# Every second attention head computed token-major, its probabilities turned by DMA, its value product four iterations later

## The chip, the cores and the metric

The kernel runs on one core of a Trainium2 chip. The metric is the device time of one execution in microseconds (us), as the median of repeated runs. The engines are named as the profile names them: PE (TensorE, matmuls), PEld (its weight loads), DVE (VectorE), ACT (ScalarE), POOL (GpSimd) and SP (SyncE, which here only issues DMAs; SPq is its queue). A matmul takes a stationary operand of 128x128 and streams a moving operand of up to 512 columns past it, into a PSUM bank of 512 f32 columns per partition. There are 8 banks.

## The reference

One transformer block with conditioning: a modulated layer norm, attention over the last 512 cached keys and values, an output projection, and a gated feed-forward part. It is cut here to the shapes that matter.

```python
# x [2048, 1024]; Hq = 32 heads of Dh = 128; 4 key/value heads; Sk = 2048; window W = 512; F = 3584; all bf16
sa, ca, ga, sb, cb, gb = split(silu(c) @ w_mod, 6)        # 6 rows of 1024
h = layernorm(x) * (1 + ca) + sa
q = (h @ wq) per head                                      # [32, 2048, 128]
k, v = last 512 rows of the caches, each shared by 8 heads
p = softmax(q @ k.T * Dh ** -0.5)                          # [32, 2048, 512]
x = x + ga * ((p @ v, heads joined) @ wo)
h = layernorm(x) * (1 + cb) + sb
x = x + gb * ((silu(h @ w_gate) * (h @ w_up)) @ w_down)
```

## The kernel before

The 2048 tokens are cut into 4 chunks of `CH` = 512 tokens. Attention runs over all chunks first, the feed-forward part follows. The residual `x_res` stays in SBUF throughout; nearly everything else lives in one arena that is carved by offsets (`arena.at`), where a new buffer takes over the pending reads and writes of those that it overlaps. A tracker (`T.op`) records the last writer and the readers of each buffer and emits the semaphore waits for them. The order of instructions on each engine is the order in which the Python code issues them; no scheduler changes it.

Attention is one loop, `for i in range(1, NA + 2)`, over `NA` = 128 heads in the order chunk, head (32 heads per chunk; head number i has chunk i // 32). It is a software pipeline. Iteration i does:

- `qproj(i + 3)`: 8 matmuls of 512 columns into bank 4 (`QB`), weights stationary, giving the query transposed (head dimension on partitions, tokens along the columns); DVE casts it to SBUF (L644).
- `scores(i - 1)`: 4 matmuls, one for each block of 128 keys, with the keys stationary and 512 query tokens moving, into banks 0 to 3. The result has keys on partitions. ACT takes the exponential of two banks at once (L813) into one of two buffers `ex_s`, 4 KB per partition.
- `pv(i - 2)`: the exponentials are the stationary operand, in pieces of 128 keys x 128 tokens, and the values with a column of ones appended are the moving one, 129 columns. 4 key blocks x 4 token blocks make 16 matmuls, into banks 5 and 6. The column of ones gives the softmax sum, and the output has tokens on partitions. DVE takes the reciprocal (L831) and scales (L834), and a DMA transpose issued from SP (L837) brings 128x512 into `oT_all`, the slot of that head.
- one step of background work (`run_bg`): the layer norm of the next chunk (statistics L424, normalisation L435, a DMA transpose of 128x1024 L454, modulation L440).
- loads: the query weights of four heads, 1 MB, every fourth iteration (`load_wq`); in chunks two and three, 24 columns of `w_mod` by DMA transposes of 256 KB (`load_mt`, L588) at the iterations of `LOADT`, each followed four iterations later by a multiply-and-sum on DVE (`mod_col`, L593).

After the last head of a chunk, `oproj` multiplies `oT_all` by the output weights: 8 blocks of 32 matmuls, 512 columns each, and DVE adds the residual by way of the `tmp` buffers (L853, L855). For the last chunk this is partly spread over the last iterations.

The feed-forward part has per chunk 28 blocks of 16 matmuls (`gateup`, with the Silu on ACT at L1059), and then `down`.

Of the kernel before, what the change touches and what calls it, by code (L numbers as in the profile page):

```python
# [3 lines left out]
ALU = mybir.AluOpType  # L4
AF = mybir.ActivationFunctionType
# [125 lines left out]
def bass_adaLN_cond__sliding_block_cached__swiglu_ffn__prompt_kernel(  # L131
# [63 lines left out]
    rstd = [rstd4[:, i:i + 1] for i in range(4)]  # L195
    bq = S_("bq", [P, 8], F32)
    rl = [S_("rl%d" % i, [P, 4], F32) for i in range(2)]
    nsc = [S_("nsc%d" % i, [P, D], BF16) for i in range(2)]
    tmp = [S_("tmp%d" % i, [P, 512], F32) for i in range(2)]

    KB = 1024
    A_BYTES = 162 * KB
# [40 lines left out]
    B_mv = [_Buf("mv%d" % i) for i in range(4)]  # L243
    B_rs = [_Buf("rs%d" % i) for i in range(4)]
    B_rl = [_Buf("rl%d" % i) for i in range(2)]
    B_ns = [_Buf("ns%d" % i) for i in range(2)]
    B_tmp = [_Buf("tmp%d" % i) for i in range(2)]
    B_h2 = [[_Buf("h2_%d_%d" % (s, dt)) for dt in range(DT)] for s in range(2)]
# [12 lines left out]
    with nc.Block() as block:  # L261

        @block.gpsimd
        def _(g):
# [5 lines left out]
            def mm(out_ap, lhsT, rhs, start, stop, reads, bank_buf, skip=False):  # L270
                T.op(PE, lambda: TE.matmul(out_ap, lhsT, rhs, start=start, stop=stop, skip_group_check=skip),  # L271
                     reads=reads, writes=[bank_buf])
# [145 lines left out]


            B_ns4 = B_ns + [_Buf("ns2"), _Buf("ns3")]  # L420
            nsc4 = [t[:, :] for t in nsc] + [arena.at(OFF_EX + (4 + 2 * i) * KB, [D], BF16, [B_ns4[2 + i]]) for i in range(2)]

            def stats(t, sl, hf):
                T.op(DVE, lambda: V.bn_stats(st_[sl][:, hf * 6:hf * 6 + 6], x_res[:, t, hf * 512:hf * 512 + 512]),  # L424
# [321 lines left out]
            for dt in range(DT):  # L746
                shift(dt)

            B_ex = [_Buf("ex%d" % i) for i in range(NEX)]
            ex_s = [arena.at(OFF_EX + i * 4 * KB, [KT, CH], BF16, [B_ex[i]]) for i in range(NEX)]  # L750
            o_s = [arena.at(OFF_OS + i * 1 * KB, [TPC, P], BF16, [B_os[i]]) for i in range(NOS)]
            oT_all = arena.at(OFF_OT, [Hq, CH], BF16, B_oT)

# [51 lines left out]
            def scores(i):  # L805
                ch, h = divmod(i, Hq)
                gk = h // rep
                qs = q_slot(i)
                es = i % NEX
                for kt in range(KT):  # L810
                    mm(bank(SCB + kt), kT_sb[:, gk * KT + kt, :], qT_s[qs], True, True, [B_kT[gk], B_qT[qs]], PB[SCB + kt])
                for kp in range(KT // 2):
                    T.op(ACT, lambda: A.activation(ex_s[es][:, 2 * kp:2 * kp + 2, :], banks2(SCB + 2 * kp), AF.Exp, scale=att_scale),  # L813
                         writes=[PB[SCB + 2 * kp], PB[SCB + 2 * kp + 1], B_ex[es]])

            def pv(i):
                ch, h = divmod(i, Hq)
                gk = h // rep
                es = i % NEX
                os_ = i % NOS  # L820

                for jj in range(2):
                    for kt in range(KT):
                        for jb in range(2):
                            j = 2 * jb + jj
                            b = PVB + jb
                            mm(bank(b, P + 1, jj * 130), ex_s[es][:, kt, j * P:(j + 1) * P], v_aug[:, gk * KT + kt, 0:P + 1],
                               kt == 0, kt == KT - 1, [B_ex[es], B_va, B_vg[gk]], PB[b])
                both = [PB[PVB], PB[PVB + 1]]
                r = i % 2  # L830
                T.op(DVE, lambda: V.reciprocal(rl[r][:, :].rearrange("p (a b) -> p a b", a=2), psap(PVB * 512 + P, [[512, 2], [130, 2]])),  # L831
                     writes=both + [B_rl[r]])
                rlb = bass.AP(tensor=rl[r][:, :].tensor, offset=0, ap=[[4, P], [2, 2], [1, 2], [0, P]])
                T.op(DVE, lambda: V.tensor_tensor(o_s[os_].rearrange("p (a b) d -> p a b d", a=2),  # L834
                                                  psap(PVB * 512, [[512, 2], [130, 2], [1, P]]), rlb, ALU.mult),
                     reads=[B_rl[r]], writes=both + [B_os[os_]])
                T.op(Q_tr[os_], lambda: SP.dma_start_transpose(oT_all[:, h, :].rearrange("p (j q) -> p j q", j=TPC),  # L837
                                                               o_s[os_].rearrange("p j d -> p (j d)")),
                     reads=[B_os[os_]], writes=[B_oT[h]])

            B_wo = [_Buf("wo%d" % i) for i in range(8)]
            wo_s = [None] * 8
# [24 lines left out]
                resid(b, t, hf * 512, 512, 0, k, x_res[:, t, :], B_x[t])  # L867
                run_bg(1)

            def oproj(ch):  # L870
                for k in range(2 * TPC):
                    b = [QB, XB][k % 2]
                    oproj_mm(ch, k, b, 0, Hq)
                    oproj_end(ch, k, b)

            ln1 = {}
            ln2 = {}
# [15 lines left out]
            GATER = {19 + n: NGP + n for n in range(DT - NGP)}  # L893
            GATET = {23: 0, 24: 1}
            GATES = {26: 0, 27: 1}
            t2 = Hq + 6 + (9 * (NL - 1)) // 4
            TURNT = (28, t2 + 1)
            PUTT = {33: (0, c_sil, B_csil), 30: (1, mrow[0:DT, :], B_mrow), t2 + 3: (2, mrow[0:DT, :], B_mrow)}
            GETT = {35: (0, sc_row, B_scr), 31: (1, rowb[0][:, :], B_row[0]), t2 + 4: (2, rowb[1][:, :], B_row[1])}
            LOADT = {Hq + 2 + (9 * n) // 4: n for n in range(NL)}  # L900
            LOADO = {5 + (21 * p) // 8: p for p in range(8)}
            LOADK = {1: 1, 5: 2, 6: 3}
            for i in range(1, NA + 2):
                ch, h = divmod(i, Hq)
                if i in LOADK:
# [27 lines left out]
                if i + LEAD < NA:  # L933
                    if (i + LEAD) % Hq == 0:
                        finish(ln1[(i + LEAD) // Hq])
                    if i == 1:
                        scores(0)
                    if i in (1, 3, 5):
                        q_bias_mm(i + 1, i + 3, XB)
                    if i > NQ0:  # L940
                        qproj(i + LEAD)
                    elif i % 2 == 1:
                        qproj_mm(NQ0 + i // 2, QB, 0, HK)
                    else:
                        qproj(NQ0 - 1 + i // 2, QB, HK)
                if i - 4 in LOADT:
                    n = LOADT[i - 4]
                    mod_col(n)
                    g0, last = divmod(n, DT)
                    if last == DT - 1:  # L950
                        mod_take(g0, B_late[g0 + 1])
                        if g0 == 1:
                            mod_gain(1, B_late[2], B_g[1])
# [2 lines left out]
                    oproj_mm(NCH - 1, 0, QB, 8 * n, 8 * n + 8)  # L956
                elif n >= 3:
                    oproj_mm(NCH - 1, 1, XB, 8 * (n - 3), 8 * (n - 3) + 8)
                if 1 <= i - 1 < NA:
                    scores(i - 1)  # L960
                if 0 <= i - 2 < NA:
                    pv(i - 2)
                    ch2, h2 = divmod(i - 2, Hq)
                    if i % 4 == 1 and i > 5:
                        load_wq((i + 4) // 4 + 1)
                    if i in LOADT:
                        load_mt(LOADT[i])
                    if h2 == Hq - 1 and ch2 < NCH - 1:
                        oproj(ch2)
                run_bg(1)  # L970
                for n in GATEP.get(i, ()):
                    gate_part(n)
                if i in GATER:
# [157 lines left out]
```

## Time and profile before

| what | value |
|---|---|
| median of 3 runs | 1270.32 us (1269.98 to 1270.42) |
| the profiled execution | 1270.14 us, span 1268.3 us |
| PE busy | 1255.1 us, 99% of the span |
| DVE, ACT, POOL busy | 485.1, 341.6, 56.0 us |
| granted TensorE clock | 1.00 |
| DMA | 156.67 MB, mean 124 GB/s |

The attention loop runs up to about 642 us of the span, with three output projections of about 55 us in it, at 142, 309 and 476 us. The profile names each instruction by its line. "Idle before" is time that the engine sat still ahead of such an instruction, with the instruction that released it. A PE that is busy 99% of the time is one whose stream of matmuls has nearly no gaps; how fast the stream goes must be read from the distance between like instructions. The DMA share is the mean busy share of the 16 DMA engines; as packets overlap it can pass 1.

### The profile page before, as it was taken

Reading aid. Unit: us, or ns where it says so; the run is one execution under the profiler, and the core shown is the slowest. Engines: PE = TensorE matmul, PEld = TensorE weight load, DVE = VectorE, ACT = ScalarE, POOL = GpSimd, SP = SyncE. Lnnn points to the kernel's source line nnn. Section 1 sums busy time; section 2 is a strip of 40 time slices with the busy share of each in tenths; the row PEclk is TensorE's granted clock in tenths of the full one; section 3 lists DMA queues with packets and bytes.
Section 4 is the critical chain, followed back from the end, with each engine's and each line's share of the span. In section 5 each row is a group of like instructions: output and inputs, shape, how many; then the busy total and the mean of one; then the engine's idle time right before and its main releaser. Section 6 shows DMA issues by size and latency. Waiting matters only on the chain.

```text
span 1268.3 us, 17609 instructions
## 1 busy us (share of the span) xinstructions
PE 1255.1 (99%) x7442; PEld 640.7 (51%) x7583; DVE 485.1 (38%) x894; ACT 341.6 (27%) x389; POOL 56.0 (4%) x95
## 2 busy tenths in 40 slices
PE   8999999999999999999999999999999999999999
PEld 5655545555455554555544444444444444444444
DVE  4676226764257641365322321233212321222122
ACT  4655205553035550155510111011100111011100
POOL 1530000000000000000000000000000000000000
PEclk9999999999999999999999999999999999999999
DMA  9998306875029641064243972055512644034200
GB/s 320 264 263 218 92 1 127 177 171 125 1 57 177 138 114 34 9 129 123 61 145 100 291 246 94 25 158 150 168 40 72 177 141 134 17 128 154 67 9 25
DMA packets 239997, 156.67 MB, mean 124 GB/s; under 512 B 133296, under 2 KB 225840, under 8 KB 239920
## 3 DMA queue, kind: packets, MB, share of 16 engines
q1 hardware_dynamic: 181664, 96.83, 31.6%
q10 hardware_dynamic: 58256, 58.73, 14.6%
q8 instruction: 59, 0.97, 0.3%
q14 instruction: 18, 0.15, 0.1%
HBM read 119.93 MB, written 4.20 MB: 98 GB/s over the span
## 4 chain that ended last, share of the span: by engine, by line
PE 98%; issue 1%; DMA 0%; SPq 0%; DVE 0%
PE ps L271 98%; DMA arena<-in_w_mod_dram 0%; SPq L309 0%; SPq L334 0%; PE ps L275 0%; DVE arena L496 0%; DVE tmp L853 0%; DVE arena L855 0%; DVE gain_f L486 0%
## 5 line engine op out<-in xcount | busy, mean ns | idle before, releaser
L271 PE MATMUL ps<-arena 128*128 128x512 bf16 (+1 forms) x7213 | 1249.3, 333 | 10.1 <-POOL arena L298 2.0
L271 PEld LDWEIGHTS ps<-arena 128*128 128x128 bf16 x7354 | 632.9, 98 | 621.5 <-issue 2.1
L813 ACT ACTIVATE arena<-ps 128x1024 bf16<-128x1024 f32 x256 | 261.9, 1023 | 345.1 <-PE ps L271 333.4
L1059 ACT ACTIVATE arena<-ps 128x512 bf16<-128x512 f32 x112 | 66.9, 597 | 499.6 <-PE ps L271 499.6
L1060 DVE TENSOR_TENSOR arena<-ps,arena 128x512 bf16<-128x512 f32 x112 | 77.5, 692 | 276.2 <-PE ps L271 276.2
L853 DVE TENSOR_TENSOR tmp<-ps,rowb 128x512 f32<-128x512 f32 (+1 forms) x65 | 44.4, 683 | 318.8 <-PE ps L271 318.8
L644 DVE CAST arena<-ps 128x512 bf16<-128x512 f32 x120 | 82.8, 690 | 47.7 <-PE ps L271 47.7
L834 DVE TENSOR_TENSOR arena<-ps,rl 128x512 bf16<-128x512 f32 x128 | 88.5, 691 | 4.7 <-DVE rl L831 0.2
L831 DVE RECIPROCAL rl<-ps 128x4 f32<-128x4 f32 x128 | 23.4, 182 | 114.1 <-PE ps L271 114.1
L429 POOL TENSOR_SCALAR rstd<-mv 128x1 f32<-128x1 f32 x28 | 6.1, 216 | 910.3 <-DVE mv L428 910.3
L424 DVE BATCH_NORM_STATS2 st<-x_res 128x6 f32<-128x512 bf16 x62 | 42.4, 683 | 3.4 <-DMA x_res<-in_A_x_dram 3.3
L593 DVE SCALAR_TENSOR_TENSOR arena<-arena 128x1024 bf16<-128x1024 bf16 x24 | 29.2, 1215 | 0.0
L855 DVE TENSOR_TENSOR arena<-tmp,x_res 128x512 bf16<-128x512 f32 (+2 forms) x33 | 22.3, 677 | 1.1
L855 DVE TENSOR_TENSOR x_res<-tmp,x_res 128x512 bf16<-128x512 f32 x32 | 22.2, 693 | 1.1
L440 DVE TENSOR_SCALAR arena<-arena,gain,mod_bf 128x512 bf16<-128x512 bf16 x56 | 21.2, 420 | 0.0
L435 DVE TENSOR_SCALAR nsc<-x_res,mv,rstd 128x1024 bf16<-128x1024 bf16 x30 | 19.2, 641 | 0.0
L431 POOL TENSOR_TENSOR rstd<-rstd,mhalf 128x1 f32<-128x1 f32 x28 | 15.7, 559 | 2.3
L772 POOL TENSOR_SCALAR arena<-arena,sc_bf 128x512 f32<-128x512 bf16 x8 | 12.9, 1614 | 0.5 <-POOL arena L774 0.2
L774 POOL TENSOR_TENSOR arena<-arena 128x512 f32<-128x512 f32 x8 | 10.1, 1265 | 0.7
L428 DVE BATCH_NORM_AGGREGATE mv<-st 128x2 f32<-128x12 f32 x28 | 5.8, 209 | 1.0
L271 PEld LDWEIGHTS ps<-sc_bf,arena 128*128 128x128 bf16 x128 | 4.4, 96 | 1.4 <-DMA arena<-in_w_mod_dram 0.3
L271 PE MATMUL ps<-sc_bf,arena 128*128 128x1 bf16 x128 | 4.7, 164 | 0.3 <-DMA arena<-in_w_mod_dram 0.3
(56 smaller groups left out, 59.4 us busy)
## 6 DMA issues: line engine op xcount, KB each, us to landing
arena<-in_A_wq_dram SPq DMA_DIRECT2D x30, 1024.0 KB, 5.8
arena<-in_B_w_gate_dram ACTq DMA_DIRECT2D x28, 1024.0 KB, 5.4
arena<-in_B_w_up_dram ACTq DMA_DIRECT2D x28, 1024.0 KB, 7.9
arena<-in_A_wo_dram SPq DMA_DIRECT2D x8, 1024.0 KB, 7.6
arena<-in_B_w_down_dram SPq DMA_DIRECT2D x7, 1024.0 KB, 8.3
out_dram<-arena SPq DMA_DIRECT2D x15, 256.0 KB, 2.0
x_res<-in_A_x_dram SPq DMA_DIRECT2D x3, 1024.0 KB, 7.0
arena<-arena SPq DMA_TRANSPOSE x132, 2.6
```

What stands on the lines that cost most here:

```text
L271: T.op(PE, lambda: TE.matmul(out_ap, lhsT, rhs, start=start, stop=stop, skip_group_check=skip), reads=reads, writes=[bank_buf])
L424: T.op(DVE, lambda: V.bn_stats(st_[sl][:, hf * 6:hf * 6 + 6], x_res[:, t, hf * 512:hf * 512 + 512]), reads=[B_x[t]], writes=[B_st[sl]])
L440: T.op(DVE, lambda: V.tensor_scalar(dst[:, dt, :], dst[:, dt, :], gain[gi][:, dt:dt + 1], mod_bf[:, ccol + dt:ccol + dt + 1], op0=ALU.mult ...
L593: T.op(DVE, lambda: V.scalar_tensor_tensor(mt[n % 2], mt[n % 2], 1.0, sc_row, op0=ALU.mult, op1=ALU.mult, accum_out=mcol[:, n:n + 1]), rea ...
L644: T.op(DVE, lambda: V.tensor_copy(qT_s[qs], bank(b)), writes=[PB[b], B_qT[qs]])
L813: T.op(ACT, lambda: A.activation(ex_s[es][:, 2 * kp:2 * kp + 2, :], banks2(SCB + 2 * kp), AF.Exp, scale=att_scale), writes=[PB[SCB + 2 * k ...
L831: T.op(DVE, lambda: V.reciprocal(rl[r][:, :].rearrange("p (a b) -> p a b", a=2), psap(PVB * 512 + P, [[512, 2], [130, 2]])), writes=both + ...
L834: T.op(DVE, lambda: V.tensor_tensor(o_s[os_].rearrange("p (a b) d -> p a b d", a=2), psap(PVB * 512, [[512, 2], [130, 2], [1, P]]), rlb, A ...
L853: T.op(DVE, lambda: V.tensor_tensor(tmp[s][:, 0:n], bank(b, n), rowb[ri][:, c0:c0 + n], ALU.mult), reads=[B_row[ri]], writes=[PB[b], B_tmp ...
L855: T.op(DVE, lambda: V.tensor_tensor(dst[:, c0:c0 + n], tmp[s][:, 0:n], x_res[:, t, c0:c0 + n], ALU.add), reads=[B_tmp[s], B_x[t]], writes= ...
L1059: T.op(ACT, lambda: A.activation(sg_s[ss], bank(gb), AF.Silu), writes=[PB[gb], B_sg[ss]])
L1060: T.op(DVE, lambda: V.tensor_tensor(guT[:, ft, :], bank(ub), sg_s[ss], ALU.mult), reads=[B_sg[ss]], writes=[PB[ub], B_gu[ft]])
```

## The change

42 heads are computed another way: the 11 even heads 2 to 22 of the second chunk (numbers 34 to 54), and the 31 even heads from 2 of the third chunk to 30 of the fourth (numbers 66 to 126). All other heads stay as they were. For such a head:

- `nat_scores`: the query is stationary, in 4 pieces of 128 tokens, and the 512 keys move. 4 matmuls of 512 columns, into the same banks 0 to 3, but with tokens on partitions and keys along the columns. ACT takes 4 exponentials, one per bank, each with the sum along its columns (`accum_out`).
- `nat_norm`, in two halves: DVE takes the reciprocals of two sums and multiplies two pieces of 128x512 in place.
- `nat_turn`: one DMA transpose from SP turns the whole head's probabilities, 128x2048, so that keys are on partitions.
- `nat_pv`, four iterations after the head's own number: for each of the 4 key blocks the values are stationary and 512 tokens move, 4 matmuls into bank 5. The result already has the head dimension on partitions, and ACT copies it into `oT_all`; no transpose of 128x512 follows.

The unturned probabilities use the place of `ex_s[0]` and the `tmp` buffers in turn; the turned ones use free places of the arena, two slots of 4 KB, at the offsets of `PTAT`. The odd heads of that stretch keep `ex_s[1]`, and heads 32 and 64 borrow the `nsc` buffer. The order in the loop is changed to go with it: scores of head i + 1 in odd iterations ahead of the value product, `load_wq` earlier in its iteration, the columns of `w_mod` at every second iteration in place of 9 in 4, and background steps left out or doubled in some iterations. At the seams (iterations 33, 65 and 97) the scores of head i + 1 stand behind the first block of `oproj`.

```diff
@@ buffers
+    psum = [S_("psum%d" % i, [P, 4], F32) for i in range(2)]
+    pinv = [S_("pinv%d" % i, [P, 4], F32) for i in range(2)]
...
+            NAT0 = Hq + 2
+            NAT = set(range(NAT0, 2 * Hq - 8, 2)) | set(range(2 * Hq + 2, NA, 2))
+            B_pn = [[_Buf("pn0_%d" % hf) for hf in range(2)], B_tmp]
+            pn = [None, tmp_t[:, :].bitcast(BF16)]
...
+            def ex_slot(i):
+                return NEX if i % Hq == 0 and i + 2 in NAT and i not in NAT else i % NEX
+
+            def p_slot(i):
+                return (i - NAT0) // 2 % 2
+
+            def pt_region(off):
+                pt_over[:] = B_oT[24:] if off == OFF_OT + 24 * KB else []
+                for s in range(2):
+                    B_pt[s] = _Buf("pt%d" % s)
+                    pt[s] = arena.at(off + s * 4 * KB, [TPC * KT, P], BF16, [B_pt[s]])
+
+            def nat_scores(i):
...
+                for j in range(TPC):
+                    mm(bank(SCB + j), qT_s[qs][:, j * P:(j + 1) * P],
+                       kT_sb[:, gk * KT:(gk + 1) * KT, :].rearrange("p a b -> p (a b)"), True, True,
+                       [B_kT[gk], B_qT[qs]], PB[SCB + j])
+                for j in range(TPC):
+                    T.op(ACT, lambda: A.activation(pn[s][:, j * 512:(j + 1) * 512], bank(SCB + j), AF.Exp, scale=att_scale,
+                                                   accum_out=psum[s][:, j:j + 1]),
+                         writes=[PB[SCB + j], B_pn[s][j // 2], B_psum[s][j // 2]])
+
+            def nat_norm(i, hf):
+                s = p_slot(i)
+                T.op(DVE, lambda: V.reciprocal(pinv[s][:, 2 * hf:2 * hf + 2], psum[s][:, 2 * hf:2 * hf + 2]),
+                     reads=[B_psum[s][hf]], writes=[B_pinv[s][hf]])
+                for j in (2 * hf, 2 * hf + 1):
+                    pj = pn[s][:, j * 512:(j + 1) * 512]
+                    T.op(DVE, lambda: V.tensor_scalar(pj, pj, pinv[s][:, j:j + 1], None, op0=ALU.mult),
+                         reads=[B_pinv[s][hf]], writes=[B_pn[s][hf]])
+
+            def nat_turn(i):
+                s = p_slot(i)
+                pt_of[i] = (pt[s], B_pt[s], list(pt_over))
+                T.op(Q_pt[s], lambda: SP.dma_start_transpose(pt[s], pn[s]), reads=B_pn[s], writes=[B_pt[s]])
+
+            def nat_pv(i):
...
+                ptv = pa.rearrange("p (j k) q -> p j k q", j=TPC)
+                for kt in range(KT):
+                    mm(bank(PVB).rearrange("p (j q) -> p j q", j=TPC), v_aug[:, gk * KT + kt, 0:P], ptv[:, :, kt, :],
+                       kt == 0, kt == KT - 1, [B_va, B_vg[gk], pb], PB[PVB])
+                T.op(ACT, lambda: A.activation(oT_all[:, h, :], bank(PVB), AF.Copy), writes=[PB[PVB], B_oT[h]])
...
-            def oproj(ch):
+            def oproj(ch, between=()):
...
+                    if k < len(between):
+                        between[k]()
...
-            t2 = Hq + 6 + (9 * (NL - 1)) // 4
+            t2 = Hq + 5 + 2 * (NL - 1)
...
-            LOADT = {Hq + 2 + (9 * n) // 4: n for n in range(NL)}
+            LOADT = {Hq + 1 + 2 * n: n for n in range(NL)}
...
+            PTAT = {NAT0: OFF_OT + 24 * KB, 2 * Hq + 2: OFF_OT + 24 * KB, 2 * Hq + 22: OFF_H20, 3 * Hq: OFF_HT}
@@ in the loop over i, behind qproj
+                if i % 4 == 1 and i >= NAT0 - 1:
+                    load_wq((i + 4) // 4 + 1)
...
+                seam = (i - 1) % Hq == 0 and i + 1 in NAT
+                if i + 1 in PTAT and not seam:
+                    pt_region(PTAT[i + 1])
+                if i in NAT and (i - 2) % Hq:
+                    nat_norm(i, 1)
+                nat = i % 2 == 1 and i + 1 in NAT
+                if nat and not seam:
+                    if i - 4 not in LOADT:
+                        run_bg(1)
+                    nat_scores(i + 1)
-                if 1 <= i - 1 < NA:
+                if 1 <= i - 1 < NA and i - 1 not in NAT:
                     scores(i - 1)
                 if 0 <= i - 2 < NA:
-                    pv(i - 2)
+                    if i - 4 in pt_of:
+                        nat_pv(i - 4)
+                    if i in NAT and (i - 2) % Hq:
+                        nat_turn(i)
+                    if i - 2 not in NAT:
+                        pv(i - 2)
+                    if (i - 2) % Hq == Hq - 1 or i == NA:
+                        for n in sorted(pt_of):
+                            if n // Hq == (i - 2) // Hq:
+                                nat_pv(n)
+                    if nat and not seam:
+                        nat_norm(i + 1, 0)
...
                     if h2 == Hq - 1 and ch2 < NCH - 1:
-                        oproj(ch2)
-                run_bg(1)
+                        oproj(ch2, [lambda: nat_scores(i + 1), lambda: (nat_norm(i + 1, 0), nat_norm(i + 1, 1))] if seam else ())
+                        if seam:
...
+                            nat_turn(i + 1)
+                if not nat or seam:
+                    run_bg(2 if i in NAT and i % 4 == 2 and i - 3 in LOADT else 1)
```

## The prediction

> **What bounds the kernel now.** I read the page first, then the timeline of the attention stage, then the rows of single lines. The page's busy table, and its chain of waits:
>
> ```profile
> span 1268.3 us, 17609 instructions
> PE 1255.1 (99%) x7442; PEld 640.7 (51%) x7583; DVE 485.1 (38%) x894; ACT 341.6 (27%) x389; POOL 56.0 (4%) x95
> PE 98%; issue 1%; DMA 0%; SPq 0%; DVE 0%
> ```
>
> TensorE is the path from end to end: a change gains only what it takes out of TensorE's stream, and costs whatever it makes TensorE wait. So I need the pitch of the matmuls. From the timeline of ACT, one exponential of the second chunk and another nine heads later, then one Silu of the feed-forward stage and another 13 column blocks later:
>
> ```profile
> 195.50 2.14 ACT L813 ACTIVATE arena<-ps 128x1024 bf16<-128x1024 f32 x2 [56.61 <-PE ps L271]
> 226.97 2.14 ACT L813 ACTIVATE arena<-ps 128x1024 bf16<-128x1024 f32 x2 [1.36 <-PE ps L271]
> ...
> 880.40 0.60 ACT L1059 ACTIVATE arena<-ps 128x512 bf16<-128x512 f32 x1 [2.86 <-PE ps L271]
> 925.29 0.60 ACT L1059 ACTIVATE arena<-ps 128x512 bf16<-128x512 f32 x1 [2.86 <-PE ps L271]
> ```
>
> Nine heads take 31.47 us, 3.497 us each, and the pitch repeats to 0.01 us: TensorE is not held up by anything there. 13 blocks of 16 matmuls of 512 columns take 44.89 us, 0.2158 us per matmul. A head is 12 of those (8 projection, 4 scores, 2.590 us) and 16 value products of 129 columns, which so cost 3.497 - 2.590 = 0.907 us, 56.7 ns each.
>
> **What the change takes from TensorE.** A token-major head replaces the 16 products by 4 matmuls of 512 columns, 0.863 us. That is 0.0436 us less per head, and 42 heads (11 and 31) give **1.83 us**. Scores stay 4 matmuls of 512 columns. Nothing else leaves TensorE, and since no stall was there, none can be won back. (The Trainium skill, "TensorE: Matmul & The Clock Gate", Back-to-back issue gap, gives an isolated gap of N/2.4 + 2.5 ns: by it 16 x 56.25 - 4 x 215.8 = 37 ns per head, 1.5 us in all, an estimate; the measured pitches decide.)
>
> **What has to fit beside it.** Odd heads stay as they were, even ones turn token-major, so the work now repeats every two heads. Zero is the start of the odd iteration's projection; TensorE's stream, by the pitches above: projection 0 to 1.73, token-major scores to 2.59, the odd head's value product to 3.50, projection to 5.22, the odd head's scores to 6.09, the value product of the token-major head of four iterations ago to 6.95 (6.99 before).
>
> *ACT.* Two exponentials of 1024 columns become four of 512 with a row sum, and a copy of the product is added. The sums' price is not in this stage; the nearest rows are the two accumulating passes of the start and the plain one-bank copy:
>
> ```profile
> 7.09 1.06 ACT L518 ACTIVATE arena<-x_res 128x1024 bf16<-128x1024 bf16 x1 [2.00 <-DMA x_res<-in_A_x_dram]
> 8.05 0.19 ACT L518 ACTIVATION_READ_ACCUMULATOR arena<-x_res 128x1 f32 x1
> ...
> L655 ACT ACTIVATE arena<-ps 128x512 f32<-128x512 f32 x4 | 2.3, 596 | 5.7 <-PE ps L271 5.7
> ```
>
> The read of 0.19 starts 0.96 into a pass of 1.06. So one costs from 0.60 - 0.10 + 0.19 = 0.69 us (overlapped) to 0.60 + 0.19 + 0.09 = 0.88 us (0.09 being the gap between the pair in L813, 2.14 less 2 x 1.023). Every second of the four waits for its predecessor, since two share a buffer, so I take 0.73, nearer the lower end. An exponential starts 0.2 us and its matmuls after the projection (cast at 299.97, exponential at 300.40), here one matmul: 2.15. Four end at 5.1 (4.9 to 5.7). The odd head's fourth score matmul needs the last bank at 5.87: 0.2 to 1.0 us to spare. Then the odd exponentials 5.85 to 7.99, the copy to 8.6, and the next four start at 9.1. ACT is filled to 5.7 of 6.95; it was 4.3 of 6.99.
>
> *DVE.* The reciprocal and scaling of an even head (0.18 + 0.69) go; two reciprocals of 128x2 (0.16 to 0.18, by L665 and L831) and four scalings of 128x512 in SBUF come (0.35 by L675, 0.42 by L440), 1.7 to 2.0 us, I take 1.8. Queued behind the new wait for the first two sums is the cast of the next projection, which frees bank 4. In order: cast 1.93 to 2.62, a modulation column 1.30 (L593) or a layer-norm step up to 0.9, the odd head's scaling to 4.7, the first two scalings to 5.5, the cast to 6.2. The projection at 6.95 needs it: 0.7 us to spare. The second half of the scalings ends at 7.1. Moving the modulation columns to every second iteration and skipping a layer-norm step beside each keeps a pair near 6.4 of 6.95 us in the second chunk; without that room the cover would be gone, at 0.1 us per 0.1 us overrun.
>
> *DMA and SP.* For 42 heads a transpose of 128x512 becomes one of 128x2048. The rows for one and for two times 128 KB:
>
> ```profile
> L837 SPq DMA_TRANSPOSE arena<-arena x128: 1188/1192/2657, 35.0 to 639.6; - x128
> DMA to landing us min/median/max: 2.4/2.6/8.1
> ...
> L454 SPq DMA_TRANSPOSE arena<-nsc x28: 1232/1250/2732, 57.0 to 1018.1; - x28
> DMA to landing us min/median/max: 3.1/5.1/7.5
> ```
>
> Alone, 128 KB more costs 0.7 us, so 512 KB land 2.4 + 3 x 0.7 = 4.5 us after issue. SP issues the turn at 7.15, held by the scalings and by the product that frees its target; queued behind it on SP are a layer-norm transpose and the next weight load, both with many us to go, and each transpose holds SP itself for 1.2 us (2.7 at most). It lands at 11.7. Two readers wait: the exponentials that refill its source two pairs on, at 16.05, and the product at 19.99. So **4.4 us of queueing** is covered. (The Trainium skill, "DMA: Bandwidth & Descriptors", Latency and other measured facts, has 261 GB/s for transposes; by it 512 KB take 2.0 us of data, an estimate, against 2.8 by the rows here, and the cover would be 0.8 us larger.)
>
> Is there that much queueing? The busiest and the quietest stretch of attention, columns PE, PEld, DVE, ACT, POOL, clock, DMA share and GB/s:
>
> ```profile
> 215.00:229.00 14.00, 13.90 (x112) 8.33 (x113) 10.73 (x22) 8.20 (x9) 0.78 (x2) 1.00 1.16 209
> 610.00:624.00 14.00, 13.89 (x111) 8.31 (x112) 6.05 (x12) 8.18 (x8) 0.00 (x0) 1.00 0.18 37
> ```
>
> The quiet one holds four small transposes: 0.18 x 14 / 4 = 0.65 us of all engines for 128 KB, 2.6 for the new kind. A 1 MB load takes 3.3 (0.35 share at 111 GB/s between 1100 and 1200 us). Per two pairs (13.9 us) with modulation columns and layer norm both running: weights 3.3, two small turns 1.3, two large 5.2, two modulation columns of 256 KB about 2.8, one layer-norm turn 1.3, in all 13.9: full. That holds for eight pairs of the second chunk, where iteration 40 adds a 1 MB load of x, and seven of the third; elsewhere it is 12.6 or less. In the stretch at 215 the small transposes already landed in 3.7 to 7.2 us, up to 4.8 late. So a few turns may come after 16.05 in the second chunk, by up to 2 us; such a delay moves the whole stream and is paid once, as it also gives the queue time. Bounds 0 to 4 us, most likely 0.4: a share of 1.16 shows that the engines overlap packets, so 13.9 is counted high.
>
> *Seams and tail.* At iterations 33, 65 and 97 scores move in between the blocks of the output projection, 55 us with a DMA share of 0.02 to 0.07: nothing. The weight load moved ahead within its iteration finds its slot already read: nothing. The last head's product comes two iterations on, at 13.9 with the turn landing at 11.7, and no loads beside it: 2.2 us to spare, nothing.
>
> **Sum.** -1.83 + 0.4 = -1.4 us. The profiled execution took 1270.14 us (span 1268.3 and 1.84 around it), 0.18 under the median of 1270.32; I give 1268.8, between 1268.7 and 1268.9.
>
> **Rivals.** What a measurement of this kernel can tell from no change is about 0.2%, 2.5 us: the forecast lies within.
>
> 1. *ACT becomes the bound (slower).* Place: bank 3, between the fourth summed exponential and the odd head's scores. It decides from (5.87 - 0.05 - 2.15) / 4 = 0.92 us per exponential. At 1.0 us, 0.32 us per pair, 42 times, 13.4 us less 1.8: 1282; at 0.95, 1273.5. For: no row shows a summed exponential from PSUM. Against: the rows bound it at 0.88. Chance 0.16.
> 2. *The turns become the bound (slower).* It decides where a turn takes over 8.9 us. If the 15 heads of the full stretches are each 0.5 us late, 7.5 less 1.8: 1276. For: the full sum above, and the delays at 215 us. Against: overlap of packets, stalls give time back. Chance 0.13, of which 0.03 stays within 2.5 us.
> 3. *The gain is eaten (no change).* Stalls of 1 to 3 us in the second chunk, or a product of 512 columns read in four pieces at a slightly longer pitch: 1269.5 to 1271.5. Chance 0.18.
> 4. *Wide matmuls gain more (faster).* If four cost less than 0.846 us, 42 heads pass 2.5 us. At 0.7 us per four, 8.7 us: 1261.6. Here 512 columns go at 0.2158 us in every stage, so the trace speaks against it. (The skill's TensorE page, same section, also states sustained 81 ns at N=128 and 131 ns at N=512; by these the change would gain over 30 us, and the measured 56.7 and 215.8 ns contradict both.) Chance 0.04.
>
> **How the numbers follow.** The forecast has 0.49. Within 0.2%: 0.49 + 0.18 + 0.03 = 0.70; slower 0.16 + 0.10 = 0.26; faster 0.04. The range runs from the full 1.83 us and a little, 1267.8, to 1278, the middle of the slower cases; left out are 0.04 below and about 0.13 above. The forecast's own range is 1268.2 to 1269.5.
>
> **What would show it.** A pair of heads in chunk three should take 6.95 us between like exponentials; a summed exponential should start 0.7 to 0.8 us after the last; the wide turns should land in 4.5 to 9 us; TensorE's waits should name neither ACT nor a transpose for more than 2 us in all. A pitch over 7.0 us, or idle of TensorE before the odd scores (ACT), before bank 4 (DVE) or of ACT before the summed exponentials (DMA), would prove the forecast wrong and name the rival.

## The result, and the profile after

The changed kernel takes 1281.02 us (median; 1280.01 to 1283.11), the kernel before 1270.32: a ratio of 1.0087, 95% interval 1.0073 to 1.0101. It is slower by 10.7 us where 1.5 us less was forecast. The profiled execution took 1281.02 us. Its page, busy table and chain:

```profile
span 1279.2 us, 17296 instructions
PE 1264.0 (99%) x7079; PEld 618.7 (48%) x7079; DVE 514.5 (40%) x1062; ACT 386.9 (30%) x683; POOL 56.0 (4%) x95
PE 92%; DMA 3%; DVE 3%; SPq 1%; ACT 0%; issue 0%; ACTq 0%
PE ps L277 92%; DMA arena<-in_A_wq_dram 3%; DVE arena L650 1%; DVE arena L896 1%; DVE arena L599 1%; DMA arena<-in_w_mod_dram 0%; DMA arena<-arena 0%; DVE arena L844 0%; DVE st L430 0%; SPq L460 0%; ACT arena L823 0%; SPq L315 0%; DVE rl L841 0%; SPq L340 0%; DVE pinv L892 0%
```

TensorE still looks 99% busy, and its busy time has grown by 8.9 us though it has less work to do: the profile counts part of a matmul's waiting as busy. The chain (what released what, followed back from the end) says more: it ran through TensorE for 98% of the span, and now for 92%. The largest of the newcomers is a DMA that had no place in it before, the load of the query weights (`in_A_wq`).

Where the time went can be read from the first residual of each chunk's output projection (L853 before, L929 after). It starts at 145.07, 312.15, 479.29 and 649.03 us before, at 145.62, 318.53, 489.53 and 660.34 after; here are those of the second chunk:

```profile
312.15 0.69 DVE L853 TENSOR_TENSOR tmp<-ps,rowb 128x512 f32<-128x512 f32 x1 [6.00 <-PE ps L271]
...
318.53 0.69 DVE L929 TENSOR_TENSOR tmp<-ps,rowb 128x512 f32<-128x512 f32 x1 [6.00 <-PE ps L277]
```

Adding the forecast saving in matmuls to the growth of each stretch gives the stalls: 0.55 us up to the first, then 5.83 + 0.48 = 6.3 in the second chunk, 3.86 + 0.65 = 4.5 in the third, 1.07 + 0.70 = 1.8 in the last. The sum of 13.1 less 1.8 is the 11.3 us that the last mark has moved. From there to the last residual of the feed-forward part (1265.5 and 1276.8 us) both kernels take 616.5 us.

Away from the stalls, the pair of heads does what was forecast. From the timeline of the last chunk, three casts two heads apart, and two summed exponentials:

```profile
577.90 0.69 DVE L650 CAST arena<-ps 128x512 bf16<-128x512 f32 x1 [1.06 <-PE ps L277]
578.12 0.60 ACT L886 ACTIVATE arena<-ps 128x512 bf16<-128x512 f32 x1 [0.61 <-PE ps L277]
...
578.90 0.60 ACT L886 ACTIVATE arena<-ps 128x512 bf16<-128x512 f32 x1
...
584.85 0.69 DVE L650 CAST arena<-ps 128x512 bf16<-128x512 f32 x1 [1.91 <-PE ps L277]
...
591.80 0.69 DVE L650 CAST arena<-ps 128x512 bf16<-128x512 f32 x1 [1.91 <-PE ps L277]
```

The pair takes 6.95 us, twice. The four exponentials start 0.78, 0.58 and 0.77 us after one another.

The stalls have two places. The first is the weight load. SP's own timeline of the second chunk, from the load of x on (duration is how long the issue held SP):

```profile
220.48 0.58 SPq L308 DMA_DIRECT2D x_res<-in_A_x_dram  x1
221.17 5.08 SPq L902 DMA_TRANSPOSE arena<-tmp  x1
226.35 1.26 SPq L460 DMA_TRANSPOSE arena<-nsc  x1
227.66 0.57 SPq L363 DMA_DIRECT2D arena<-in_A_wq_dram  x1
...
242.66 0.57 SPq L363 DMA_DIRECT2D arena<-in_A_wq_dram  x1
243.28 1.31 SPq L847 DMA_TRANSPOSE arena<-arena  x1
244.64 2.59 SPq L594 DMA_TRANSPOSE arena<-in_w_mod_dram  x1
247.33 3.06 SPq L902 DMA_TRANSPOSE arena<-arena  x1
250.44 1.27 SPq L847 DMA_TRANSPOSE arena<-arena  x1
251.76 1.30 SPq L594 DMA_TRANSPOSE arena<-in_w_mod_dram  x1
253.17 2.15 SPq L902 DMA_TRANSPOSE arena<-tmp  x1
255.41 1.57 SPq L460 DMA_TRANSPOSE arena<-nsc  x1
257.03 0.57 SPq L363 DMA_DIRECT2D arena<-in_A_wq_dram  x1
```

From one weight load to the next, four iterations, SP is held 0.57 + 1.31 + 2.59 + 3.06 + 1.27 + 1.30 + 2.15 + 1.57 = 13.8 of 14.4 us: SP is held nearly all the time. Between the same two loads of the kernel before (iterations 45 and 49, at 237.53 and 251.51 us) its holds come to 12.2 of 14.0 us, so there was little room. A wide turn (L902) holds SP 2 to 3 us, and 5.08 us behind the load of x. The load that should leave at the start of iteration 41, about 218 us, leaves at 227.66, and TensorE reaches its weights before they have landed (idle in brackets):

```profile
233.58 5.12 PEld L277 LDWEIGHTS ps<-arena 128*128 128x128 bf16 x37 [1.51 <-DMA arena<-in_A_wq_dram]
```

The same happens at 248, 262, 419 and 434 us. Each time the load of the weights is the one that TensorE waits for, not a turn. The second place is bank 5, at 284, 480 and 644 us; the first of these:

```profile
283.35 2.14 ACT L823 ACTIVATE arena<-ps 128x1024 bf16<-128x1024 f32 x2 [0.64 <-PE ps L277]
285.38 0.59 ACT L913 ACTIVATE arena<-ps 128x512 bf16<-128x512 f32 x1
286.03 11.17 PE L277 MATMUL ps<-arena 128*128 128x129 bf16 x93 [1.42 <-ACT arena L913]
```

The value product of head 56 follows that of head 54 at once and writes the same bank, whose copy (L913) stands on ACT behind two exponentials.

### The profile page after: what moved, and what is told of

The parts are those of the page before. It is cut to its first block, busy times and chain, and to the rows that moved or that the text cites. A ratio compares the mean times of both kernels' runs of the same rounds, so it can differ in the third digit from the quotient of the medians.

```text
span 1279.2 us, 17296 instructions
## 1 busy us (share of the span) xinstructions
PE 1264.0 (99%) x7079; PEld 618.7 (48%) x7079; DVE 514.5 (40%) x1062; ACT 386.9 (30%) x683; POOL 56.0 (4%) x95
## 3 DMA queue, kind: packets, MB, share of 16 engines
q10 hardware_dynamic: 58256, 58.73, 14.4%
## 4 chain that ended last, share of the span: by engine, by line
PE 92%; DMA 3%; DVE 3%; SPq 1%; ACT 0%; issue 0%; ACTq 0%
PE ps L277 92%; DMA arena<-in_A_wq_dram 3%; DVE arena L650 1%; DVE arena L896 1%; DVE arena L599 1%; DMA arena<-in_w_mod_dram 0%; DMA arena<-arena 0%; DVE arena L844 0%; DVE st L430 0%; SPq L460 0%; ACT arena L823 0%; SPq L315 0%; DVE rl L841 0%; SPq L340 0%; DVE pinv L892 0%
## 5 line engine op out<-in xcount | busy, mean ns | idle before, releaser
L277 PEld LDWEIGHTS ps<-arena 128*128 128x128 bf16 x6818 | 609.1, 98 | 654.3 <-DMA arena<-in_A_wq_dram 7.9
L823 ACT ACTIVATE arena<-ps 128x1024 bf16<-128x1024 f32 x168 | 171.9, 1023 | 238.7 <-PE ps L277 231.0
L1166 ACT ACTIVATE arena<-ps 128x512 bf16<-128x512 f32 x112 | 66.9, 597 | 500.2 <-PE ps L277 500.2
L929 DVE TENSOR_TENSOR tmp<-ps,rowb 128x512 f32<-128x512 f32 (+1 forms) x65 | 44.4, 683 | 318.6 <-PE ps L277 318.6
L886 ACT ACTIVATE arena<-ps 128x512 bf16<-128x512 f32 x88 | 52.1, 595 | 46.2 <-PE ps L277 37.3
L844 DVE TENSOR_TENSOR arena<-ps,rl 128x512 bf16<-128x512 f32 x86 | 59.5, 692 | 3.0
L886 ACT ACTIVATE tmp<-ps 128x512 bf16<-128x512 f32 x80 | 47.4, 595 | 18.4 <-PE ps L277 14.8
L841 DVE RECIPROCAL rl<-ps 128x4 f32<-128x4 f32 x86 | 15.7, 183 | 67.3 <-PE ps L277 67.2
L896 DVE TENSOR_SCALAR arena<-arena,pinv 128x512 bf16<-128x512 bf16 x88 | 31.1, 354 | 3.1
L896 DVE TENSOR_SCALAR tmp<-tmp,pinv 128x512 bf16<-128x512 bf16 x80 | 28.3, 354 | 2.8
L913 ACT ACTIVATE arena<-ps 128x512 bf16<-128x512 f32 x42 | 24.9, 592 | 4.6 <-PE ps L277 4.6
L886 ACT ACTIVATION_READ_ACCUMULATOR arena<-ps 128x1 f32 x88 | 17.3, 196 | 0.0
```

The source lines that it names most:

```text
L886: T.op(ACT, lambda: A.activation(pn[s][:, j * 512:(j + 1) * 512], bank(SCB + j), AF.Exp, scale=att_scale, accum_out=psum[s][:, j:j + 1]), ...
L896: T.op(DVE, lambda: V.tensor_scalar(pj, pj, pinv[s][:, j:j + 1], None, op0=ALU.mult), reads=[B_pinv[s][hf]], writes=[B_pn[s][hf]])
L929: T.op(DVE, lambda: V.tensor_tensor(tmp[s][:, 0:n], bank(b, n), rowb[ri][:, c0:c0 + n], ALU.mult), reads=[B_row[ri]], writes=[PB[b], B_tmp ...
L1166: T.op(ACT, lambda: A.activation(sg_s[ss], bank(gb), AF.Silu), writes=[PB[gb], B_sg[ss]])
```

## The experiments

Each was timed beside the kernel before on the same chip; that kernel's medians were 1270.29 to 1270.39 us. Times are medians, with the lowest and highest run.

### Who is late: the loads on another queue, the banks, the loads ahead

**e1_act_queue**

```diff
-                if i % 4 == 1 and i >= NAT0 - 1:
-                    load_wq((i + 4) // 4 + 1)
...  behind nat_scores(i + 1); True: issued by ACT
+                if i % 4 == 1 and i >= NAT0 - 1:
+                    load_wq((i + 4) // 4 + 1, True)
```

> The query-weight loads from iteration 33 on are issued from ACT's queue instead of SP's; all else is the changed kernel (1281.0 us). Theory A (order on SP: a 1 MB load stands behind turns that hold SP while their ring is full): the five waits of TensorE for weights, 6.1 us in the profiled run, and the short waits that follow them, some 2 us, go: 1273 to 1275 us, and the loads are issued within 1 us of the iteration's scores. Rival B (the 16 DMA engines are full, and a load is late wherever it is issued): the waits for weights stay within 2 us of 6.1, 1279 us or more.

Measured: 1279.0 us (1276.4 to 1281.0), ratio 1.0067 (1.0052 to 1.0082). Neither theory as stated. The waits for weights went, down to 0.7 us, as A said; but one large wait came in their place in the profiled execution, the slowest of the four. The timeline just behind the load of x, which left at 218.19:

```profile
218.88 6.69 SPq L904 DMA_TRANSPOSE arena<-tmp  x1
222.26 0.37 ACTq L365 DMA_DIRECT2D arena<-in_A_wq_dram  x1
...
232.84 0.60 ACT L888 ACTIVATE tmp<-ps 128x512 bf16<-128x512 f32 x1 [6.42 <-DMA arena<-tmp]
233.59 0.61 PE L277 MATMUL ps<-arena 128*128 128x512 bf16 x1 [3.31 <-ACT tmp L888]
```

The turn issued at 218.88 landed after 13.9 us. The exponentials that refill its source waited 6.4 us for it, and TensorE 3.3 us for them. So the loads no longer stand in SP's order, but a turn that they overlap in time is late instead. The Trainium skill, "DMA: Bandwidth & Descriptors", Rules for kernel authors, says that spreading DMAs over issuing engines doesn't help, as all run on the same 16 DMA engines, and saves issue time only; this run agrees, with 1279.0 us against 1281.0.

**e2_banks**

```diff
-                        nat_pv(i - 4)
+                        nat_pv(i - 4, PVB if i - 2 in NAT else XB)
...
-                                nat_pv(n)
+                                nat_pv(n, PVB + 1 if i == NA else XB)
```

> Only the bank of three value products is changed (heads 54 and 94 into bank 7, head 126 into bank 6), the changed kernel otherwise. Theory C (these three are followed or preceded at once by another product in bank 5, so TensorE waits for a copy on ACT that is queued behind two exponentials, or for a scaling on DVE): the gaps of 1.8, 1.1 and 1.9 us at 284, 480 and 644 us go: 1276 to 1277 us. Rival D (the gaps are only where a delay of the loads shows, and move on to another place): less than 1.5 us is won, 1279.5 us or more.

Measured: 1276.83 us (1275.8 to 1277.7), ratio 1.0051 (1.0036 to 1.0066), 4.2 us less than the changed kernel. The three gaps are gone from the trace, those for weights stay. Theory C holds: 4.2 of the 13.1 us came from two products that follow each other in one bank.

**e3_load_ahead**, and **e4_ahead_banks** with the banks of e2 as well

```diff
-                if i % 4 == 1 and i >= NAT0 - 1:
-                    load_wq((i + 4) // 4 + 1)
+                if i % 4 == 0 and i >= NAT0 - 2:
+                    load_wq(i // 4 + 2)
```

> The query-weight loads stay on SP but are issued one iteration earlier, at iterations divisible by four behind their projection, so that they stand ahead of that iteration's wide turn and layer-norm turn. Theory A: the loads leave SP about 5 to 8 us earlier and land before TensorE asks: 1273 to 1276 us. Rival B: the engines are full all the same, and what the loads win the wide turns lose: 1278 us or more, with waits of ACT for a turn in place of those for weights.

> The earlier loads and the other banks together. Theories A and C: the gains add, some 6 to 8 and 4.5 us: 1268.8 to 1271.5 us; what stays is the 1.3 us wait behind DVE at 377 us and small ones. Rivals B or D: 1275 us or more.

Measured: 1292.64 us (ratio 1.0179, 1.0162 to 1.0196) and 1288.06 us (1.0140, 1.0125 to 1.0155). A miss for theory A, e3 11.6 us worse than the change itself. No wait for weights is left. The wide turn of e3 has two sources in turn; the one from `tmp`:

```profile
L902 SPq DMA_TRANSPOSE arena<-tmp x20: 1876/5040/7565, 205.9 to 642.7; - x20
...
DMA to landing us min/median/max: 4.2/5.3/10.2
```

Of the 20 turns from `tmp` nearly all now stand behind a 1 MB load. They hold SP for 5.0 us, against 2.0 in the changed kernel, land up to 10.2 us after issue, and TensorE waits 8.1 us in 19 places for the exponentials behind them. So the order decides which of the two is late; one of them is. That agrees with rival B for the second and third chunk, where all these waits are; in the last chunk five of the seven turns from `tmp` hold SP for 4.1 to 5.8 us as well, and nothing waits for them. e4 is e3 less 4.6 us: the banks add as in e2.

### What fills SP: the load of x, the second chunk, the turns, the columns

**e5_x_later**

```diff
-            LOADX = {19: 2, 40: 3}
+            LOADX = {19: 2, 58: 3}
```

> Only the 1 MB load of x is moved, from iteration 40 (among the wide turns of the second chunk) to iteration 58 (behind them). Theory E (this load puts SP behind, since the next wide turn then holds SP for 5 us, and SP has no spare time to catch up): the waits for weights at 232, 248 and 262 us go with the short ones behind them, 5 to 6 us: 1275 to 1276.5 us. Rival F (SP is over-full by itself while modulation columns and layer norm run beside the wide turns): at most the first of the three goes, 1279 us or more.

Measured: 1278.5 us (1277.1 to 1279.7), ratio 1.0064 (1.0049 to 1.0079), between the two. In the profiled execution the wait at 232 us went, those at 246, 260 and 275 stayed. The load of x starts the delay, but waits for weights remain without it, as rival F says. That is one execution, the slowest of the four; e8 below, which is the same kernel up to iteration 58, shows another.

**e7_no_second**

```diff
-            NAT = set(range(NAT0, 2 * Hq - 8, 2)) | set(range(2 * Hq + 2, NA, 2))
+            NAT = set(range(2 * Hq + 2, NA, 2))
```

> The 11 heads of the second chunk stay in the old form; the 31 others are token-major as in the changed kernel. Theory: the second chunk lost 6.3 us between its projections against an expected gain of 0.5, so without it 1281.0 - 6.3 + 0.5 = 1275 us (1274 to 1276). If its stalls only move to the third chunk: 1278 us or more.

Measured: 1275.57 us (1275.1 to 1276.4), ratio 1.0042 (1.0027 to 1.0057). As expected: the 11 heads cost 5.5 us, and their stalls don't move on to the third chunk.

**e9_turns_alone**, the wide turns in the kernel before

```diff
+                if i in WIDE:            # even heads 34-54, 66-86, 96-126
+                    T.op(Q_pt[n], lambda: SP.dma_start_transpose(pt[n], x_res[:, 0:2, :].rearrange("p a b -> p (a b)")),
+                         reads=[B_os[os_]] + B_x[0:2], writes=[B_pt[n]])
...
+                    return
                 T.op(Q_tr[os_], lambda: SP.dma_start_transpose(oT_all[:, h, :]...
```

> The kernel before with nothing changed but this: 38 even heads (11, 11 and 16 in the last three chunks) issue a turn of 128x2048, of rows of x into spare places, instead of their own turn of 128x512; so these outputs are not turned, and no instruction waits for the wide turns. Theory G (the wide turns by themselves fill SP and the DMA engines so far that a weight load comes late): waits of TensorE for weights in the second chunk, 1 to 6 us, and SP held 2 to 5 us by a wide turn: 1271.5 to 1276 us. Rival H (it takes the changed order of loads and modulation columns too): no such waits, 1270.0 to 1271.0 us.

Measured: 1279.42 us (1278.9 to 1279.8), ratio 1.0068 (1.0055 to 1.0081): theory G, and by more than expected. No order, engine or bank is changed here, no instruction of the trace waits for these turns, and the kernel before becomes 9.1 us slower:

```profile
L839 SPq DMA_TRANSPOSE arena<-x_res x38: 1582/2893/5982, 204.7 to 646.7; - x38
DMA to landing us min/median/max: 4.2/5.1/8.7
...
PE ps L271 <- DMA arena<-in_A_wq_dram: 7.0, 4, 5.3
```

TensorE waits 7.0 us for weights in four places, 5.3 of it in one; a lower clock behind that one costs about 2.1 us more (last section), which makes the 9.1. The turns hold SP much as in the changed kernel, 1.6 to 6.0 us.

**e12_half_turn**, and **e15_no_columns**

```diff
-                T.op(Q_pt[s], lambda: SP.dma_start_transpose(pt[s], pn[s]), reads=B_pn[s], writes=[B_pt[s]])
+                T.op(Q_pt[s], lambda: SP.dma_start_transpose(pt[s][:, 0:8, :], pn[s][:, 0:1024]), reads=B_pn[s], writes=[B_pt[s]])
```

```diff
             def load_mt(n):
+                if n > 1:
+                    return
```

> The changed kernel, with only the first half of each head's probabilities turned (128x1024 in place of 128x2048, so the value products read stale data for the rest). Theory G: with 256 KB less per pair of heads SP is free again, and the waits for weights (6.1 us) and the short ones behind them go, the three bank waits (4.8 us) and the one behind DVE (1.3) stay: 1273 to 1275 us. Rival I (SP is late because it waits for the scalings on DVE, whatever the turn's size): 1278.5 us or more.

> The changed kernel with 22 of the 24 modulation columns not loaded (their sums are taken of stale data). If it is the sum of all the traffic that is too much in the second and third chunk: no waits for weights and few for turns, the bank waits and the one behind DVE stay, 1273 to 1275 us, like the half turn. If a wide turn beside a 1 MB load is late whatever else runs: waits at the load of x (about 230 us) and at weights stay, 3 us or more: 1277 us or more.

Measured: 1274.09 us (1273.9 to 1274.6; ratio 1.0027, 1.0017 to 1.0038) and 1274.09 us (1274.0 to 1274.5; ratio 1.0030, 1.0019 to 1.0041). Both hit, and to the same time, 6.9 us below the changed kernel. With half the turn, SP is held 1.24 us by it; without the columns the turns hold SP as long as ever (medians 1.9 and 3.0 us), but there is room. No wait for weights is left inside the token-major stretches of either. What TensorE still waits for there in e12:

```profile
PE ps L277 <- ACT arena L913: 2.9, 2, 1.5
...
PE ps L277 <- DVE arena L844: 1.1, 1, 1.1
PE ps L277 <- DVE pinv L892: 0.9, 1, 0.9
```

the three banks, and one wait behind DVE. So it is the sum of the traffic, not the turn next to a load alone, and not a wait of SP for DVE (rival I). Both runs relieve SP and the 16 DMA engines together, so they don't tell which of the two is full.

### What is left when the stalls are taken out

**e13_half_banks**: e12 with the banks of e2 and

```diff
-                    run_bg(2 if i in NAT and i % 4 == 2 and i - 3 in LOADT else 1)
+                    run_bg(2 if i in NAT and i % 4 == 2 and i - 3 in LOADT and i != 2 * Hq + 2 else 1)
```

> The half turn of the earlier run (the second half of the probabilities isn't turned) with the other banks and one layer-norm step instead of two at iteration 66. If the forecast's matmul term was right and the turns, the banks and that step are all that went wrong, nothing but 0.5, 0.4, 0.6 and 0.3 us of short waits is left of the stalls: 1270.36 - 1.83 + 1.8, corrected for their part that the kernel before also has (0.4), 1269.5 to 1270.1 us by the gaps as counted; 1268.5 to 1269.2 if short gaps are mostly an artefact of counting weight loads. If the four wide matmuls are dearer than thought, or ACT or DVE hold the pair of heads: 1271 us or more.

Measured: 1269.31 us (1268.9 to 1271.1), ratio 0.9994 (0.9985 to 1.0003), between the two ranges expected; the interval includes no change. 4.8 us below e12, and 1.0 below the kernel before: the saving of 1.83 us, less the short waits that the trace still has at 144, 204, 370 and 530 us. In this run nothing in ACT, DVE or the wide matmuls holds the pair of heads up.

**e6_four_edits** (e1, e2, e5 and the step of e13) and **e8_x_banks** (e6 without e1)

> Weights from ACT's queue, x at iteration 58, the three products in other banks, and one layer-norm step instead of two at iteration 66. If the stalls found so far are all, what stays is the saving in matmuls, 1.83 us, less about 1 us of short waits at 144, 203 and 540 us: 1268.6 to 1269.8 us, faster than the kernel before (1270.36). If the wide turns are too much for the DMA engines in any case, waits of the summed exponentials for a turn appear in their place: 1272 us or more.

> As the run with four edits, but the weights stay on SP in the order of the changed kernel. Theory A with E: the waits for weights in the third chunk (419 and 434 us, no load of x near) stay, 2.4 us and short ones behind them, while the second chunk is free of them: 1271 to 1273 us, 2 to 3.5 us above the run with four edits. If the load of x was all: within 0.7 us of that run.

Measured: 1270.32 us (1269.1 to 1273.1; ratio 1.0001, 0.9991 to 1.0010) and 1270.78 us (1270.1 to 1275.5; 1.0010, 1.0000 to 1.0020). e6 lies between its two ranges: its best four runs are at 1269.1 to 1269.3, its others up to 1273, and the profiled one, 1273.06, has turns late at 264, 279 and 413 us. The order of weights on SP or ACT makes no clear difference (0.5 us), which e8's theory of 2 to 3.5 us missed. In e8's profiled execution (1270.21 us) no wait for weights is left in either chunk, and one turn is late, at 264 us. Up to iteration 58 that is the kernel of e5, whose profiled execution waited three times: without the load of x the second chunk is at the edge, and executions differ. Why the waits of the third chunk went too isn't shown.

**e10_load_at_head** (e6, but ACT issues the weights ahead of the exponentials) and **e11_head_31** (the same without the second chunk's heads, x at iteration 40)

> All 42 heads; banks, x at iteration 58 and the layer-norm step as in the run with four edits; the weights come from ACT's queue at the start of their iteration, ahead of the summed exponentials, which is right behind a wide turn and not ahead of one, and at the seams from SP as in the kernel before. If a turn is late only where a 1 MB load stands just ahead of it: no waits for turns or weights but under 1 us in all, 1268.6 to 1269.6 us. If the second chunk is too full in any order: 1270 us or more.

> As the run before it, but the second chunk in the old form (31 heads, expected saving 1.35 us) and x loaded at iteration 40 as in the kernel before. With the second chunk's crowding gone and 0.3 to 0.6 us of short waits left: 1269.2 to 1269.8 us, and a narrower spread from run to run than with 42 heads. If the third chunk, where 8 modulation columns and the layer norm still run, is too full as well: 1270 us or more.

Measured: 1276.2 us (1272.6 to 1280.7; ratio 1.0045, 1.0027 to 1.0062) and 1271.06 us (1269.8 to 1272.2; 1.0003, 0.9994 to 1.0012). Both miss their first range and fall under the second: turns are late in the stretches with columns and layer norm, in this order too (at 244 and 427 us in e10, at 396 us in e11).

**e16_31_ln_late**: 31 heads, the banks of e2, the second chunk's loads as in the kernel before, and the last layer norm behind the columns

```diff
-                if h == 2 and 1 <= ch < NCH - 1:
+                if (i == Hq + 2 and NCH > 2) or i == 2 * Hq + 14:
                     add_ln1(ch + 1)
...
-                    run_bg(2 if i in NAT and i % 4 == 2 and i - 3 in LOADT else 1)
+                    run_bg(2 if i in NAT and 2 * Hq + 14 <= i < 3 * Hq else 1)
```

> 31 heads (none in the second chunk), the other banks, weights on SP with the second chunk's loads at the place of the kernel before, and the layer norm of the last chunk begun at iteration 78 instead of 66, so that it runs behind the modulation columns and not beside them. If the stalls come from the sum of the traffic, the third chunk now has at most 12.6 us of it per 13.9 us and no weight or turn is late: 1270.3 - 1.35 + 0.3 to 0.6 = 1269.2 to 1269.6 us, all runs within 0.5 us, faster than the kernel before. If 12.6 is still too much, or the layer norm crowds DVE behind: 1270.3 us or more, with a wide spread.

Measured: 1269.11 us (1268.8 to 1270.8), the kernel before 1270.31 (1270.0 to 1270.6), ratio 0.9992 (0.9983 to 1.0001). That is 0.1 us below the range given, on the side that was expected; the spread is wider than the 0.5 us expected, 0.7 us and one run at 1270.75. The interval just reaches 1, but ten of its eleven runs lie below the fastest of the fifteen of the kernel before. The wide turns hold SP as long as in the changed kernel (medians 1.9 and 3.0 us), and no wait for a turn or for weights is left. Of the versions that compute everything this is the fastest.

## Why the prediction was wrong, step by step

- **The matmul term was right.** A pair takes 6.95 us, as forecast, and the medians of e13 and e16 lie below the kernel before by about what the term leaves after the short waits (e16: 1.35 expected for 31 heads, 1.2 measured).
- **ACT and DVE were right.** A summed exponential takes 0.71 us on average (0.73 forecast), a scaling 0.354 (0.35 to 0.42). Rival 1 did not come.
- **The step on SP failed, and it cost most: 0.4 us was put down for queueing, some 7 came.** It said that what stands behind the turn on SP, a layer-norm transpose and the next weight load, has "many us to go", and priced the hold of SP at "1.2 us (2.7 at most)" per transpose. That was read from transposes of 128 and 256 KB; the wide ones hold SP 2.0 to 3.0 us (medians), 5.2 at most. Summed over four iterations SP has 13.8 of 14.4 us taken, a sum the prediction never made, though it made the one for the 16 engines. The load due at the start of iteration 41 left about 9 us late, 4.4 us before TensorE's weight loads ran dry (at 232.07), and landed after 5.9; none of these loads lands in under 5.5.
- **"Paid once" failed with it.** The bounds of 0 to 4 us took a delay to give the queue time. With SP held nearly all the time it came back: five weight loads were late, and with the short waits behind them that is some 7 us (e12 and e15 against the change: 6.9).
- **The deadline was watched at the wrong reader.** The turn's landing was priced well (4.5 us; 4.4 is the median), and its cover of 4.4 us of queueing was not used up: no turn took over 7.2 us to land in the changed kernel, against 8.9 allowed. (The Trainium skill, "DMA: Bandwidth & Descriptors", Latency and other measured facts, gives the 261 GB/s that the prediction quotes for a non-contiguous middle dimension only; the sum did not use it.) The weights, which nothing in the change touches but their place in the queue, had less. Rival 2 had the right side, and its 7.5 us of stalls is near the 6.9 found, but by luck: it took late turns as the cause, and it was the weights.
- **"Seams and tail: nothing" failed.** The deadline of the last turn was checked there, the bank was not. Three products meet another in bank 5 (iterations 58, 97 and 128): 4.2 us (e2). "Nothing" for the moved load failed by 0.5 us too: at iteration 33 it stands ahead of the turn of head 31, which the output projection waits for at 144 us; in e16, with this load behind that turn, the wait is gone.
- **A term was missing on DVE.** At iteration 66 two layer-norm steps and the end of a modulation group fall together ahead of a cast: 0.9 us by TensorE's wait, 0.3 with one step less (e13). With the 6.9, 4.2 and 0.5 above it makes 12.5 of the 13.1 us; short waits of 0.4 to 0.5 us, at 204 and 541, are about the rest.

What stays open: why a wide turn holds SP that long, by itself and behind a load. The runs show that the hold goes with the turn's size (1.24 and 2 to 3 us) and with a load just ahead (5.0), not what SP waits for; that a full ring is what holds it, as the theory of e1 has it, no run shows. Nor is it shown whether SP or the 16 DMA engines behind it are the first to be full: from 253 to 267 us the engines' share is 1.12, where the kernel before has 0.62, so both are busier.

## What to carry to other kernels

Before a DMA is made four times larger, sum the time that its queue's issuer is held per period, not only the bytes: where the issuer is held nearly all the time, whatever stands behind comes late, and the first to suffer may be a load that the change does not touch. Follow every PSUM bank through the irregular iterations, where two uses come together that the steady loop keeps apart. And when all of the work already hides behind one engine, a saving of 0.1% is worth less than the spare time of the queues that pay for it.

## What the runs showed of the hardware

A wait of several us costs more than itself. In e9 TensorE stood still for 5.3 us, from 232.3 to 237.6; windows in it and after it (columns PE, PEld, DVE, ACT, POOL, clock, DMA share, GB/s):

```profile
234.00:235.00 1.00, 0.00 (x0) 0.00 (x0) 0.96 (x3) 0.00 (x0) 0.00 (x0) 0.99 0.89 301
235.00:236.00 1.00, 0.00 (x0) 0.00 (x0) 0.17 (x1) 0.00 (x0) 0.66 (x2) 0.50 1.07 362
...
239.00:242.00 3.00, 3.00 (x9) 1.02 (x8) 0.69 (x1) 0.00 (x0) 0.00 (x0) 0.53 0.67 134
242.00:246.00 4.00, 3.95 (x34) 2.41 (x34) 2.02 (x4) 2.51 (x3) 0.00 (x0) 1.00 1.04 202
```

The granted clock fell to 0.50 within the wait and stayed there for about 4 us after it: some 10 matmuls at 0.43 us instead of 0.216, another 2.1 us. Waits of 1 to 2 us, as in the changed kernel, left it at 1.00. The Trainium skill, "TensorE: Matmul & The Clock Gate", Part 1, has the half rate after an idle window of about 3.4 us and the full one after as long a busy one. The half rate is what these traces show; but the drop came sooner, 2.7 us into the wait here and 2.4 us in e1 (whose wait lasted 3.3 us), and the return here some 4.2 us after TensorE went on. On the times the measurement decides.
